# Attention with normalised q and k, then a gated MLP: another timing for the preparation of q and k and for their loads

## The chip, the cores and the metric

The kernel runs on one core of one Trainium2 chip. The metric is the device time of one execution in microseconds; the median of three executions of the kernel before was 333.86 (331.49 to 334.69). Profiles are single executions under the hardware profiler. The granted clock is the share of TensorE's full clock that it was given; the DMA share is the mean busy share of the core's 16 DMA engines as the profile counts it, and it goes above 1. PE is TensorE's matmuls and PEld its weight loads, DVE is VectorE, ACT is ScalarE, POOL is GpSimd, SP is SyncE, which here only issues transfers. An execution counts as slow when it lies more than 1.5% above the fastest execution of the same kernel in the same rounds.

## The reference, cut to what matters

```python
# q, k, v: 8 batches x 12 heads x 448 tokens x 64, float32
def rmsnorm(x, g):
    rms = np.sqrt(np.mean(x * x, axis=-1, keepdims=True) + 1e-06)
    return x / rms * g
q_n, k_n = rmsnorm(q, g_q), rmsnorm(k, g_k)
attn = softmax(q_n @ k_n.T / sqrt(64))          # per head
x = (attn @ v), heads side by side              # 8 x 448 x 768
h = relu(x @ w_in)                              # 768 x 1024
u, v = halves of h;  v_n = layernorm(v)
v_s = w_spatial @ v_n + b_spatial               # over tokens
out = (u * v_s) @ w_out                         # 512 x 768
```

## The kernel before

Each batch is cut into three groups of four heads, 24 groups in all. Raw q and k are loaded, squared, summed, turned into a scale by a logarithm and an exponential on ACT, multiplied by it, and transposed. From then on the kernel is one clock of steps. A step computes two passes of scores on PE into a single tile of PSUM and ends in one exponential on ACT; a group takes 3.5 steps. The first 20 passes go one at a time ("early passes" p0 to p19); then come steps 10 to 83, and a tail. Group G is first needed at step 3.5 G. I call "step s" the moment at which its exponential starts.

```python
def squares(*key, eng=None):                      # GpSimd, or ACT where asked
    ...
    if eng is act:
        act.activation(out=t, in_=x, func=AF.Square, bias=0.0, scale=1.0)
    else:
        pool.tensor_tensor(out=t, in0=x, in1=x, op=ALU.mult)

def reduce(*key):                                 # DVE: sum of squares -> "ms"
    dve.tensor_reduce(out=sqs[gk][:, key[1], :], in_=..., axis=AX.X, op=ALU.add)

def rstd(*gk):                                    # ACT: "ln", then "rs"
    act.activation(out=ln, in_=t, func=AF.Ln, bias=eps, scale=1.0 / D)
    act.activation(out=rst[gk], in_=ln, func=AF.Exp, bias=0.0, scale=-0.5)

def scaled(*key, eng=None):                       # GpSimd, or DVE: "n"
    (eng or pool).tensor_tensor(out=..., in0=raw[key], in1=<scale, broadcast>, op=ALU.mult)

def transpose_dma(G, i):                          # on SyncE's queue: "qT", "kr"
    sync.dma_start_transpose(out=..., in_=nrm[G, i]...)

def k_scale(G):                                   # DVE, once k's transpose has landed: "kT"
    dve.tensor_scalar(out=t, in0=krs.pop(G), scalar1=g2_col, ..., accum_out=tot)

# ... cut: loads; q and k of batches 0 and 1 come group by group ("qf", "kf": 4 pieces each),
# those of batches 2 to 7 a whole batch at a time ("qb", "kb": 4 pieces each), all on SyncE's queue

EVEN = {-8: ("sq", 0), -7: ("sq", 1), -6: ("red",), -5: ("rstd",), -4: ("sc", 1), -1: ("ks",)}
ODD = {-6: ("sq", 0), -5: ("sq", 1), -4: ("red",), -3: ("rstd",), -2: ("sc", 1), 2: ("ks",)}
# ... for G >= 6: step 7 * (G // 2) + offset, one or two later for G < 8
for b in range(2, B):
    s0 = max(S0 + 2 if b == 2 else 17, NCH * NG * b // 2 - 17)
    for n in range(8):
        at(s0 + n // (2 if b < 4 else 1), NG * b, "ld", n)

for s in range(S0, NST):
    scores(pss[:, 0:2], 2 * s)                    # PE
    scores(pss[:, 2:4], 2 * s + 1)
    prep(s, True)                                 # ACT's logarithms, before the exponential
    expo(pss, 2 * s, 2)
    prep(s, False)                                # squares, sums, scales, transposes, loads
    # ... cut: v, w_out; attention of a finished group, or units of the MLP
```

In these traces ACT, GpSimd and SyncE each take their instructions in the order of the program. So a logarithm that waits holds the next exponential (3.40 us before the one at 175.43 us in the prediction's third fence), and a square that waits holds all of GpSimd's later work (3.76 us before the one at 172.59).

## Time and profile before

| read from the profile before | value |
|---|---|
| span of the profiled execution | 333.2 us |
| first exponential / step 10 | 11.79 / 44.46 us |
| step 24 | 100.95 us |
| step 43 / step 83 | 163.51 / 302.01 us |

The starts of the exponentials are the best ruler for this kernel, since every cause of delay must show in one of them. In the lines of a timeline the first number is the start in microseconds, the second the duration, then engine, source line, operation, output and input; the bracket is the idle time of the engine just before, and what ended it. In the view of waits a line says who waited for whom, the sum in microseconds, how often, and the longest. The lines themselves are in the prediction below.

| line in the timelines | what it is |
|---|---|
| L249 | square on GpSimd |
| L257, L265, L266 | sum on DVE; logarithm and exponential that make the scale |
| L276 | multiplication by the scale |
| L340, L346 | transposing transfer; the copy of k's transpose on DVE |
| L366, L373 | scores; the step's exponential |
| L90 to L93 / L105 | load of a group / of a part of a batch |

### The profile page before, as it was taken

Reading aid. Unit: us, or ns where it says so; the run is one execution under the profiler, and the core shown is the slowest. Engines: PE = TensorE matmul, PEld = TensorE weight load, DVE = VectorE, ACT = ScalarE, POOL = GpSimd, SP = SyncE. Lnnn points to the kernel's source line nnn. Section 1 sums busy time; section 2 is a strip of 40 time slices with the busy share of each in tenths; the row PEclk is TensorE's granted clock in tenths of the full one; section 3 lists DMA queues with packets and bytes.
Section 4 is the critical chain, followed back from the end, with each engine's and each line's share of the span. In section 5 each row is a group of like instructions: output and inputs, shape, how many; then the busy total and the mean of one; then the engine's idle time right before and its main releaser. Section 6 shows DMA issues by size and latency. Waiting matters only on the chain.

```text
span 333.2 us, 6464 instructions
## 1 busy us (share of the span) xinstructions
PE 281.5 (84%) x2537; PEld 131.0 (39%) x2537; DVE 200.3 (60%) x340; ACT 212.5 (64%) x276; POOL 205.3 (62%) x183
## 2 busy tenths in 40 slices
PE   7568779739759999779977989989959989999994
PEld 7333333314314444334433434334334434444552
DVE  5784645543648394495655585586756566745652
ACT  3637766827646877658656768767755776675411
POOL 4576795659976697379545896499464990120210
PEclk9977979978997999999995999999987999999999
DMA  4999897998991999839977999589946397131155
GB/s 124 223 209 229 154 132 162 191 205 123 182 231 27 205 213 244 172 79 152 237 170 93 228 201 232 107 143 179 280 59 108 35 201 79 26 94 49 25 144 165
DMA packets 82944, 50.90 MB, mean 153 GB/s; under 512 B 46753, under 2 KB 79170, under 8 KB 82914
## 3 DMA queue, kind: packets, MB, share of 16 engines
q1 hardware_dynamic: 67218, 41.53, 61.9%
q0 software_dynamic: 15408, 8.73, 20.1%
q8 instruction: 20, 0.33, 0.4%
q10 hardware_dynamic: 288, 0.23, 0.3%
q14 instruction: 10, 0.08, 0.1%
HBM read 38.55 MB, written 11.01 MB: 149 GB/s over the span
## 4 chain that ended last, share of the span: by engine, by line
PE 32%; POOL 21%; DMA 18%; DVE 10%; issue 8%; ACT 7%; SPq 4%; POOLq 0%; DVEq 0%; ACTq 0%
POOL sqt L249 10%; DMA kb<-in_k_dram 10%; PE ps L395 8%; PE ps L526 6%; DMA kr<-n 5%; POOL n L276 5%; PE ps L467 4%; PE ps L507 4%; ACT et L373 4%; PE ps L497 3%; PE pss L366 3%; POOL vt L130 3%; DVE ms L257 3%; POOL vn L489 3%; DMA qb<-in_q_dram 2%
## 5 line engine op out<-in xcount | busy, mean ns | idle before, releaser
L373 ACT ACTIVATE et<-pss 128x1792 bf16<-128x1792 f32 x74 | 122.8, 1660 | 46.4 <-PE pss L366 42.8
L410 DVE TENSOR_TENSOR xt<-ps,rc 128x448 bf16<-128x448 f32 x48 | 28.1, 620 | 63.1 <-ACT rc L403 50.5
L366 PE MATMUL pss<-qT,kT 64*128 64x448 bf16 x254 | 38.9, 363 | 20.5 <-DVE kT L346 16.3
L257 DVE TENSOR_REDUCE ms<-sqt 128x14 f32<-128x896 f32 x46 | 48.2, 1076 | 11.3 <-POOL sqt L249 10.6
L395 PE MATMUL ps<-et,vt 128*32 128x448 bf16 x768 | 45.1, 374 | 8.6 <-DVE osb L444 7.0
L526 PE MATMUL ps<-w_out,gt 128*128 128x384 bf16 (+1 forms) x256 | 48.5, 333 | 0.3 <-DVE gt L511 0.3
L467 PE MATMUL ps<-w_in_v,xt 128*128 128x512 bf16 (+1 forms) x192 | 48.7, 393 | 0.0
L249 POOL TENSOR_TENSOR sqt<-kb 128x896 f32<-128x896 f32 x18 | 30.3, 1684 | 23.6 <-DMA kb<-in_k_dram 18.2
L497 PE MATMUL ps<-xt,w_in_u 128*128 128x448 bf16 x192 | 43.0, 369 | 1.2 <-ACT vs L436 0.7
L276 POOL TENSOR_TENSOR n<-qb,rs 128x896 bf16<-128x896 f32 x18 | 30.5, 1696 | 20.3 <-ACT rs L266 20.2
L346 DVE TENSOR_SCALAR_CACHE_REDUCE kT<-kr,g_col 128x896 bf16<-128x896 bf16 x20 | 22.7, 1137 | 22.7 <-DMA kr<-n 22.7
L395 PEld LDWEIGHTS <-vt 128*32 128x32 bf16 x768 | 23.2, 101 | 25.7 <-issue 11.7
L526 PEld LDWEIGHTS <-gt 128*128 128x128 bf16 (+1 forms) x256 | 24.6, 102 | 20.8 <-issue 7.1
L366 PEld LDWEIGHTS <-kT 64*128 64x128 bf16 x276 | 10.5, 94 | 53.1 <-issue 30.2
L444 DVE COPY osb<-ps 128x384 f32<-128x384 f32 (+1 forms) x45 | 24.4, 555 | 10.8 <-PE ps L526 7.8
L249 POOL TENSOR_TENSOR sqt<-qb 128x896 f32<-128x896 f32 x18 | 30.3, 1684 | 0.7 <-DMA qb<-in_q_dram 0.6
L276 POOL TENSOR_TENSOR n<-kb,rs 128x896 bf16<-128x896 f32 x18 | 30.4, 1691 | 0.0
L507 PE MATMUL ps<-w_spT,vn 128*128 128x448 bf16 (+1 forms) x128 | 27.2, 353 | 2.3 <-DVE w_spT L222 2.3
L485 POOL TENSOR_SCALAR nm<-mv 128x4 f32<-128x4 f32 x8 | 1.9, 237 | 43.7 <-DVE mv L476 43.6
L489 POOL TENSOR_SCALAR vn<-vs,nm,rv 128x512 bf16<-128x512 bf16 (+1 forms) x32 | 24.1, 768 | 5.4 <-ACT rv L484 4.4
L497 PEld LDWEIGHTS <-w_in_u 128*128 128x128 bf16 x192 | 17.9, 101 | 24.0 <-issue 11.5
L467 PEld LDWEIGHTS <-xt 128*128 128x128 bf16 (+1 forms) x192 | 18.2, 103 | 20.4 <-issue 6.5
(92 smaller groups left out, 354.3 us busy)
## 6 DMA issues: line engine op xcount, KB each, us to landing
out_dram<-osb SPq DMA_DIRECT2D x55, 192.0 KB, 3.9
qb<-in_q_dram SPq DMA_DIRECT2D x12, 384.0 KB, 5.8
kb<-in_k_dram SPq DMA_DIRECT2D x12, 384.0 KB, 7.2
qb<-in_q_dram SPq DMA_DIRECT2D x12, 288.0 KB, 6.5
kb<-in_k_dram SPq DMA_DIRECT2D x12, 288.0 KB, 7.3
vt<-in_v_dram POOLq DMA_DIRECT2D x16, 192.0 KB, 5.4
vt<-in_v_dram POOLq DMA_DIRECT2D x16, 144.0 KB, 5.0
qf<-in_q_dram SPq DMA_DIRECT2D x10, 128.0 KB, 4.6
```

What stands on the lines that cost most here:

```text
L249: pool.tensor_tensor(out=t, in0=x, in1=x, op=ALU.mult)
L257: dve.tensor_reduce(out=sqs[gk][:, key[1], :], in_=sqt.pop(key).rearrange("p h c d -> p (h c) d"), axis=AX.X, op=ALU.add)
L276: (eng or pool).tensor_tensor(out=t.rearrange("p c h d -> p h c d"), in0=raw[key], in1=rst[gk][:, key[1], :].rearrange("p (h c) -> p h c", ...
L366: pe.matmul(out=ps[:, h, 0:S], lhsT=kT[r, c0:c0 + 128], rhs=qT[r, :], start=True, stop=True, tile_position=(64 * h, 0))
L373: act.activation(out=ets[s][:, 2 * a:2 * a + 2 * m, :], in_=ps[:, 0:2 * m, 0:S], func=AF.Exp, bias=0.0, scale=1.0)
L395: pe.matmul(out=ps[32 * l:32 * l + 32, 0:S], lhsT=w, rhs=et_of(G, 3 if r == 3 else r + 4 * y, h), start=(r == 0), stop=(r == 3), tile_posi ...
L410: dve.tensor_tensor(out=xts[b][:, 2 * g + half, :], in0=pst.pop((G, half))[:, 0:S], in1=rec[G], op=ALU.mult)
L467: pe.matmul(out=ps[0:m, :], lhsT=xts[b][:, j, t0:t0 + m], rhs=w_in_v[:, j, :], start=(j == 0), stop=(j == 5), tile_position=(0, 0))
L489: pool.tensor_scalar(out=vn_t[b % 2][0:m, c, :], in0=vs[b][c][0:m, :], scalar1=nms[b][0:m, c:c + 1], scalar2=rvs[b][0:m, c:c + 1], op0=ALU ...
L497: pe.matmul(out=ps[:, 0:S], lhsT=w_in_u[:, j, 128 * f:128 * f + 128], rhs=xts[b][:, j, :], start=(j == 0), stop=(j == 5))
L507: pe.matmul(out=ps[:, 0:S], lhsT=vn_t[b % 2][0:kp, c, 128 * f:128 * f + 128], rhs=w_spT[0:kp, c, :], start=(c == 0), stop=(c == NT - 1))
L526: pe.matmul(out=ps[o:o + m, 0:384], lhsT=gts[b][f][:, t0:t0 + m], rhs=w_out[:, f, r], start=(f == 0), stop=(f == 3), tile_position=(0, o))
```

## The change

The intent: GpSimd should never get two squares in one step; batch 2 joins batches 0 and 1 in being loaded group by group; the order of the first groups' work is written out by hand; the loads of the other batches get more lead. The lines of the timelines keep their numbers.

```diff
-    load_first(1, 1, sync)
+    load_first(1, 1, act)
...
         if p == 0:
-            squares(1, 0, eng=act)
             squares(1, 1)
             load_v(0, range(4))
+            load_w_in(1)
+            squares(2, 1)
+            load_w_in(0)
...
+        elif p == 1:
+            squares(1, 0, eng=act)
...
         elif p == 3:
             rstd(1)
             scaled(1, 0, eng=dve)
             scaled(1, 1, eng=dve)
-            squares(2, 0)
-            squares(2, 1)
-            load_w_in(1)
+        elif p == 4:
+            squares(2, 0, eng=act)
...
+    EVEN = {"sq": (-11, -8), "red": (-9, -7), "rstd": (-6,), "sc": (-6, -5), "tr": (-5, -4), "ks": (-1,)}
+    ODD = {"sq": (-9, -7), "red": (-6, -5), "rstd": (-3,), "sc": (-3, -2), "tr": (-2, -1), "ks": (2,)}
+    FIRST = {4: {...}, 5: {"sq": (10, 11), "red": (11, 12), "rstd": (13,), "sc": (13, 14), "tr": (14, 14), "ks": (16,)},
+             6: {"sq": (13, 14), "red": (14, 15), "rstd": (16,), "sc": (16, 17), "tr": (17, 17), "ks": (20,)},
+             7: {"ldg": (12, 12), "sq": (15, 17), ..., "tr": (19, 20), "ks": (23,)},
+             8: {"ldg": (15, 15), "sq": (18, 20)}}
...
+    SC8 = 23
+    for b in range(3, B):
+        first_q = max(15 if b == 3 else SC8 + 1, (21 * b - 38) // 2)
+        for n in range(4):
+            todo.setdefault(first_q + n // 2, []).append(("ld", NG * b, n))
+            todo.setdefault(first_q + 2 + (n if b % 2 == 0 else n // 2), []).append(("ld", NG * b, n + 4))
```

The first lines move two transfers, the second half of the first k, from SyncE's queue to ACT's. The pairs are steps for q and for k. "ldg" loads a group of batch 2, "ld" a quarter of a batch's q or k. Within a step, transposes are issued before loads. Also cut: group 6 is loaded in the early passes 16 and 17, v of batch 1 is issued in pass 9 instead of 15, the loads of whole batches use their two buffers in the other order, and the buffers of the start are given up in step 24 instead of 17.

## The prediction

> **What bounds the kernel now.** I read the page first, then ACT's rows in order of time, and for each long gap all engines around it. The lines of the page that matter are the busy shares, the DMA row and the chain that ended last:
>
> ```profile
> span 333.2 us, 6464 instructions
> ...
> PE 281.5 (84%) x2537; PEld 131.0 (39%) x2537; DVE 200.3 (60%) x340; ACT 212.5 (64%) x276; POOL 205.3 (62%) x183
> ...
> PE 32%; POOL 21%; DMA 18%; DVE 10%; issue 8%; ACT 7%; SPq 4%; POOLq 0%; DVEq 0%; ACTq 0%
> ...
> L373 ACT ACTIVATE et<-pss 128x1792 bf16<-128x1792 f32 x74 | 122.8, 1660 | 46.4 <-PE pss L366 42.8
> ```
>
> No engine is full. PE looks it at 84%, but only 32% of the chain is PE; 39% is GpSimd plus DMA, which mostly prepare q and k. The kernel is a clock of 84 steps, each ending in an exponential on ACT. From step 10 (start 44.46 us) to step 83 (302.0) there are 73 steps in 257.5 us, 3.53 us each. Undisturbed runs of steps are shorter: the exponentials at 151.51 and 163.51 are four steps apart, 3.0 us each, and there PE works almost without a gap. So 3.0 us is what PE asks for, and the other 0.53 x 73 = 39 us are stalls. ACT idles 46.4 us before these 74 exponentials; this counts short waits too. The long gaps on ACT that I can name: 5.01 us at 20 us, 7.15 at step 17, 2.56 at step 20, 4.47 at step 24, 2.88 at step 35, then 3.40 + 2.58 at steps 46 and 47 and, one period of two batches later, 3.49 + 2.58 at steps 67 and 68. Sum 34.1 us. Three kinds, one of each:
>
> ```profile
> 17.33 4.55 DVE L276 TENSOR_TENSOR n<-qf,rs 128x896 bf16<-128x896 f32 x1 [0.80 <-ACT rs L266]
> 17.56 1.74 POOL L249 TENSOR_TENSOR sqt<-qf 128x896 f32<-128x896 f32 x1
> ...
> 19.20 1.73 POOL L249 TENSOR_TENSOR sqt<-kf 128x896 f32<-128x896 f32 x1
> ...
> 21.81 1.08 DVE L276 TENSOR_TENSOR n<-kf,rs 128x896 bf16<-128x896 f32 x1
> ...
> 25.24 1.73 ACT L373 ACTIVATE et<-pse 128x896 bf16<-128x896 f32 x2 [5.01 <-PE pse L366]
> ```
>
> This is the timeline (start, duration). The same DVE multiplication takes 1.08 us alone and 4.55 beside two GpSimd squares: it ends just after they do. Group 1's transposes wait for it.
>
> ```profile
> 62.95 3.36 SPq L340 DMA_TRANSPOSE kr<-n  x1
> ...
> 71.21 1.15 DVE L346 TENSOR_SCALAR_CACHE_REDUCE kT<-kr,g_col 128x896 bf16<-128x896 bf16 x1 [7.29 <-DMA kr<-n]
> ...
> 73.02 1.67 ACT L373 ACTIVATE et<-pss 128x1792 bf16<-128x1792 f32 x1 [7.15 <-PE pss L366]
> ```
>
> Second kind: group 5's transposed k is issued in the step that consumes it, and lands 8.3 us after its issue (71.21 - 62.95), behind the big loads of batches 2 and 3.
>
> ```profile
> 164.10 0.65 SPq L105 DMA_DIRECT2D kb<-in_k_dram  x1
> ...
> 172.59 1.68 POOL L249 TENSOR_TENSOR sqt<-kb 128x896 f32<-128x896 f32 x1 [3.76 <-DMA kb<-in_k_dram]
> ...
> 175.43 0.32 ACT L265 ACTIVATE ln<-ms,eps 128x28 f32<-128x28 f32 x1 [3.40 <-DVE ms L257]
> ```
>
> Third kind: the last part of batch 5's k leaves SyncE at 164.10, two steps before its square; square, sum and logarithm follow in series, and ACT holds the next exponential behind the logarithm.
>
> **What the skill says.** "SBUF — State Buffer", section "Who interferes with whom": a VectorE instruction with two SBUF inputs contends with a GpSimd instruction that reads SBUF, and the second to issue waits the first out. The 4.55 against 1.08 us agree. "DMA: Bandwidth & Descriptors", section "Issuing engines are not separate DMA queues": all queues end on the same 16 engines, so another issuer saves only issue time. Here a SyncE issue is about 0.61 us. The same page, "Queues, rings and completion order": each ring is consumed in order, so a transpose issued after loads waits behind them; the 8.3 us of k's transpose beside a median of 4.7 for such transposes agree. "Perfetto Trace Analysis", "Identifying the Most-Contended Engine", warns that matmul busy time and the occupancy of 16 DMA engines both mislead; indeed the windows view gives DMA shares above 1, up to about 1.2 in its fullest 10 us.
>
> **The change, part by part.** No computation is added; squares, sums and transposes are the same in number. One square (group 2's q) goes from GpSimd to ACT: 0.95 us (the same form at 13.46) there instead of 1.7 on GpSimd.
>
> 1. Start. Two first loads go to ACT's queue: SyncE's later loads leave 2 x 0.61 = 1.2 us earlier. Group 1's q square on ACT moves behind exponential 1, which removes its 0.77 us wait for data, but the k square still ends about 15.0, so group 1's scale is still ready at 17.3. Then the two DVE multiplications find GpSimd only issuing loads (15.0 to 19.9; at 21.81 such issuing did not stretch DVE): 2 x 1.09 instead of 4.55 + 1.08. Saved: 5.63 - 2.18 = 3.4 us, all on the path. The first attention moves one exponential later and both halves of w_in load some 3 to 12 us earlier, which I count as nothing. With earlier arrivals up to step 10: 4 us.
>
> 2. Steps 10 to 24. Batch 2's groups 6, 7, 8 come in small loads (128 and 96 KB a piece) in the order of need, and group 5 is scaled in steps 13 and 14 rather than 14 and 15, transposed in 14, used in 16: two steps (6 us) for k's transpose instead of none. Group 6's transposes move from step 19 to 17 (used in 20), group 7's from 21 to 19 and 20 (used in 23). Against 7.15 + 2.56 + 4.47 = 14.2 us of stalls I would expect 10 to 12 back if DMA were free. It isn't: the window 0 to 101 us has shares of 0.96, 1.03 and 0.99, some 100 us of sixteen engines' work. At 1.2 the same work takes 83 us, so step 24 (100.95 now) cannot come much before 85. Part 1's 4 us and this part together would ask for 85 to 87, with no slack. I take 6 us here, so 10 in sum, step 24 at about 91.
>
> 3. Steps 24 to 43. Even groups are summed, normalized and transposed a step earlier: three steps from k's transpose to its use rather than two, 9 us against the 7.4 us that group 10's took (127.59 to 135.00). That removes most of 2.88; with fewer short waits 3 us.
>
> 4. Steps 43 to 83. In odd batches k's last part is issued at step 36 instead of 42 (21 steps later for batch 7), and group 15's k is squared in step 42 instead of 44: six steps of room instead of two. That removes 3.40 + 3.49 and the 2 x 2.58 that follow from them (DVE, late by the sum, frees PE's banks late): 12.0 us. Squares and sums now sit singly in their steps (at most two GpSimd operations of 1.69 in a 3.0 us step), but GpSimd stays an in-order engine with 3 us of LayerNorm and 4 issues of v a batch, so I leave 1 us for new waits: 11 us.
>
> Sum: 10 + 3 + 11 = 24 us of 334; predicted 310. As a check, steps 24 to 83 would take 201 - 14 = 187 us for 59 steps, 3.17 each, still above 3.0.
>
> The tail after step 83, 31 us, is untouched.
>
> **Rivals.** *DMA becomes the bound.* For it: shares near 1 until 236 us; queues 61.9% + 20.1% of the span are 273 us of work that the change does not lessen. At 1.2 that is 228 us at least, and most of it must come before step 64. Against: the windows 235.8 to 333 have shares from 0.67 to 0.37, and between 137 and 163 it is 0.86, so from step 24 on there is room. If it bites through the first half, only the end of part 4 and part 1 remain: 320 to 325.
>
> *The stalls return as other waits.* The outputs stand in SyncE's queue before loads and transposes and wait for DVE's copies (51.2 us in 7 waits at one of these lines), and the logarithm of each group still blocks ACT if GpSimd is late: square to logarithm stays two steps for even groups. That would eat half: about 321.
>
> *Everything goes.* All 34 us named return, and PE, less often idle, keeps a higher clock (granted 0.91 in the stalled stretch from 163.5, 1.00 in the next): about 300. DMA speaks against it.
>
> **Range and chances.** Between the third rival and the first: 300 to 323. 2% of 333.86 is at 327.2; to stay above it two thirds of the named stalls would have to remain or be replaced. I give 0.87 to faster, 0.11 to the same and 0.02 to slower, since no work is added.
>
> **What would show it.** In the profile after: group 1's two DVE multiplications at about 1.1 us each and no 5 us gap near 20 us (part 1); step 17's gap below 3 us and step 24 near 91 (part 2); no logarithm that waits over 3 us after 160 us, and kb's last loads landed before their squares (part 4); ACT's idle before the 74 exponentials down from 46.4 to about 25. DMA shares of 1.1 and more in every window up to 90 us, with transposes landing 8 us late, would show the first rival; new waits of ACT's logarithms or of the transposes behind outputs the second. If step 24 stays near 100 or if steps 43 to 83 still take over 132 us (138.5 now), the prediction is wrong.

## The result, and the profile after

The changed kernel took 318.7 us in the median of three executions (317.55 to 318.87). The ratio of the mean of its fast executions to the mean of the fast executions of the kernel before in the same rounds is 0.9551 (95% interval 0.9467 to 0.9635); being a ratio of means over a selection, it is not quite the ratio of the medians. All ratios below are computed so. The time is inside the predicted range, 8.7 us above the 310 us predicted. The profiled executions differ by 333.2 - 316.8 = 16.4 us, where I had predicted 24.

These are lines of the page of the changed kernel: span, busy shares, the chain that ended last, and the exponentials with ACT's idle time before them.

```profile
span 316.8 us, 6478 instructions
...
PE 276.5 (87%) x2527; PEld 128.3 (40%) x2537; DVE 197.4 (62%) x340; ACT 212.2 (67%) x277; POOL 203.6 (64%) x182
...
PE 39%; POOL 15%; DMA 14%; DVE 12%; ACT 9%; SPq 5%; issue 5%; POOLq 0%; DVEq 0%; ACTq 0%
...
L373 ACT ACTIVATE et<-pss 128x1792 bf16<-128x1792 f32 x74 | 122.9, 1660 | 52.2 <-PE pss L366 48.8
```

GpSimd and DMA, 39% of the chain before, are 29% now, and PE has grown from 32 to 39%. The idle time before the exponentials did not fall: 52.2 us against 46.4. The view of waits says where it went. First before, then after:

```profile
ACT ln L265 <- DVE ms L257: 24.4, 18, 3.5
DVE kT L346 <- DMA kr<-n: 22.7, 8, 7.3
POOL sqt L249 <- DMA kb<-in_k_dram: 18.2, 5, 6.5
```

```profile
DVE ms L257 <- POOL sqt L249: 17.3, 8, 3.9
...
POOL sqt L249 <- DMA kb<-in_k_dram: 9.6, 1, 9.6
DVE kT L346 <- DMA kr<-n: 9.5, 2, 6.8
ACT ln L265 <- DVE ms L257: 7.0, 7, 1.8
```

Logarithms used to stop ACT for 24.4 us in 18 waits; now it is 7.0. An idle moment that began before a logarithm now begins before the exponential that follows, so the sum in the exponential's row is no measure of what was gained. The starts of the exponentials are. The table subtracts them in the two profiles.

| | before | after | gain so far | gain of the part | predicted |
|---|---|---|---|---|---|
| step 10 | 44.46 | 44.38 | 0.1 | 0.1 | 4 |
| step 24 | 100.95 | 97.65 | 3.3 | 3.2 | 6 |
| step 43 | 163.51 | 159.73 | 3.8 | 0.5 | 3 |
| step 83 | 302.01 | 285.66 | 16.4 | 12.6 | 11 |
| end | 333.16 | 316.79 | 16.4 | 0.0 | 0 |

**The start.** The timeline of the changed kernel from 14.5 us on, group 1's squares and multiplications:

```profile
15.10 1.67 POOL L249 TENSOR_TENSOR sqt<-kf 128x896 f32<-128x896 f32 x1 [4.59 <-DMA kf<-in_k_dram]
...
18.54 1.09 DVE L276 TENSOR_TENSOR n<-qf,rs 128x896 bf16<-128x896 f32 x1 [0.64 <-ACT rs L266]
...
19.33 2.32 POOL L198 DMA_DIRECT2D w_in_v<-in_moe_w_in_dram  x4
...
19.55 2.57 DVE L276 TENSOR_TENSOR n<-kf,rs 128x896 bf16<-128x896 f32 x1
...
24.48 2.54 ACT L373 ACTIVATE et<-pse 128x896 bf16<-128x896 f32 x3 [2.71 <-PE pse L366]
```

The first multiplication is down from 4.55 to 1.09 us, as intended. But the k square starts at 15.10, where before it started at 13.30, since its data landed later. And the second multiplication takes 2.57 us beside GpSimd's issues of w_in (19.33 to 21.65). The early pass p7 comes at 24.48 instead of 25.24. The first attention, now a pass later, moves its gap with it (p9 to p10 took 3.22 us before, p10 to p11 takes 2.98 now), so compare around it: p11 is 1.0 us ahead (30.35 against 31.35), p19 0.8. Of that, 0.7 is lost before step 10, where the sum of group 4's q now stands in the way (a wait of 1.35 us before, 2.06 after).

**Steps 16 to 21.** The timeline from 58 to 88 us:

```profile
60.09 1.24 SPq L340 DMA_TRANSPOSE kr<-n  x1
...
66.00 1.66 ACT L373 ACTIVATE et<-pss 128x1792 bf16<-128x1792 f32 x1
66.34 0.60 SPq L93 DMA_DIRECT2D kf<-in_k_dram  x1
66.99 2.61 SPq L105 DMA_DIRECT2D qb<-in_q_dram  x4
...
72.99 3.48 SPq L340 DMA_TRANSPOSE kr<-n  x1
...
83.80 1.15 DVE L346 TENSOR_SCALAR_CACHE_REDUCE kT<-kr,g_col 128x896 bf16<-128x896 bf16 x1 [6.81 <-DMA kr<-n]
...
85.99 1.66 ACT L373 ACTIVATE et<-pss 128x1792 bf16<-128x1792 f32 x1 [7.36 <-PE pss L366]
```

The exponential at 66.00 is step 17, and its wait of 7.15 us is gone: group 5's k was issued at 60.09, two steps ahead. At step 20 the kernel is 8.4 us ahead (76.96 against 85.38). Then a wait of the old size stands in another place, step 21 at 85.99: group 6's k was issued at 72.99 and had landed only when DVE took it at 83.80, 10.8 us later. Ahead of it in SyncE's queue are four loads of batch 3's q ("qb", x4) and the loads of group 8. The windows view of the changed kernel gives, for a stretch of time, its length, then busy time of PE, PEld, DVE, ACT and GpSimd with counts, the granted clock, the DMA share and GB/s:

```profile
44.00:66.00 22.00, 20.19 (x169) 7.74 (x171) 14.05 (x24) 17.22 (x23) 17.35 (x13) 0.84 0.64 140
66.00:85.40 19.40, 12.03 (x114) 5.51 (x113) 7.61 (x13) 9.64 (x12) 17.61 (x16) 0.84 1.31 183
```

The DMA share is 0.64 just before group 6's transposes are issued, and 1.31 while they are awaited. The granted clock is 0.62 from 85.4 to 90.6 us, just after this wait, and step 22 took 4.71 us.

**Steps 43 to 48.** The timeline from 160 us on:

```profile
167.09 0.32 ACT L265 ACTIVATE ln<-ms,eps 128x28 f32<-128x28 f32 x1
167.76 1.66 ACT L373 ACTIVATE et<-pss 128x1792 bf16<-128x1792 f32 x1
...
171.50 1.66 ACT L373 ACTIVATE et<-pss 128x1792 bf16<-128x1792 f32 x1 [1.03 <-PE pss L366]
```

The logarithm before step 46 no longer waits (3.40 us before), and step 47 waits 1.03 instead of 2.58 us. Steps 46 and 47 took 6.04 and 5.27 us before, 2.71 and 3.74 now; steps 67 and 68 repeat it, 6.13 and 5.26 before, 2.71 and 3.74 now.

### The profile page after: what moved, and what is told of

It is laid out like the page before. It is cut to its first block, busy times and chain, and to the rows that moved or that the text cites. A ratio compares the mean times of both kernels' runs of the same rounds, so it can differ in the third digit from the quotient of the medians.

```text
span 316.8 us, 6478 instructions
## 1 busy us (share of the span) xinstructions
PE 276.5 (87%) x2527; PEld 128.3 (40%) x2537; DVE 197.4 (62%) x340; ACT 212.2 (67%) x277; POOL 203.6 (64%) x182
## 4 chain that ended last, share of the span: by engine, by line
PE 39%; POOL 15%; DMA 14%; DVE 12%; ACT 9%; SPq 5%; issue 5%; POOLq 0%; DVEq 0%; ACTq 0%
PE ps L526 10%; PE ps L467 7%; POOL sqt L249 6%; ACT et L373 6%; PE ps L507 6%; PE pss L366 6%; PE ps L395 6%; DMA kb<-in_k_dram 4%; POOL n L276 4%; PE ps L497 4%; DVE ms L257 4%; DMA qf<-in_q_dram 3%; POOL vn L489 3%; DMA kf<-in_k_dram 2%; DMA kr<-n 2%
## 5 line engine op out<-in xcount | busy, mean ns | idle before, releaser
L373 ACT ACTIVATE et<-pss 128x1792 bf16<-128x1792 f32 x74 | 122.9, 1660 | 52.2 <-PE pss L366 48.8
L257 DVE TENSOR_REDUCE ms<-sqt 128x14 f32<-128x896 f32 x46 | 49.3, 1075 | 17.9 <-POOL sqt L249 17.3
L467 PE MATMUL ps<-w_in_v,xt 128*128 128x512 bf16 (+1 forms) x182 | 45.4, 381 | 0.4
L395 PE MATMUL ps<-et,vt 128*32 128x448 bf16 x768 | 44.1, 369 | 1.7 <-ACT lr L402 1.7
L276 POOL TENSOR_TENSOR n<-qb,rs 128x896 bf16<-128x896 f32 x15 | 25.4, 1693 | 25.4 <-ACT rs L266 25.3
L497 PE MATMUL ps<-xt,w_in_u 128*128 128x448 bf16 x192 | 40.3, 354 | 0.8 <-ACT vs L436 0.8
L366 PEld LDWEIGHTS <-kT 64*128 64x128 bf16 x276 | 10.8, 94 | 51.3 <-issue 31.1
L249 POOL TENSOR_TENSOR sqt<-kb 128x896 f32<-128x896 f32 x15 | 25.1, 1682 | 9.6 <-DMA kb<-in_k_dram 9.6
L395 PEld LDWEIGHTS <-vt 128*32 128x32 bf16 x768 | 21.3, 101 | 20.0 <-issue 6.4
L507 PE MATMUL ps<-w_spT,vn 128*128 128x448 bf16 (+1 forms) x128 | 28.1, 364 | 0.1
L497 PEld LDWEIGHTS <-w_in_u 128*128 128x128 bf16 x192 | 17.3, 98 | 21.2 <-issue 7.5
L276 POOL TENSOR_TENSOR n<-kb,rs 128x896 bf16<-128x896 f32 x15 | 25.4, 1693 | 0.1
L249 POOL TENSOR_TENSOR sqt<-qb 128x896 f32<-128x896 f32 x15 | 25.2, 1678 | 0.0
```

Source lines behind the costliest of these rows:

```text
L257: dve.tensor_reduce(out=sqs[gk][:, key[1], :], in_=sqt.pop(key).rearrange("p h c d -> p (h c) d"), axis=AX.X, op=ALU.add)
L276: (eng or pool).tensor_tensor(out=t.rearrange("p c h d -> p h c d"), in0=raw[key], in1=rst[gk][:, key[1], :].rearrange("p (h c) -> p h c", ...
L366: pe.matmul(out=ps[:, h, 0:S], lhsT=kT[r, c0:c0 + 128], rhs=qT[r, :], start=True, stop=True, tile_position=(64 * h, 0))
L373: act.activation(out=ets[s][:, 2 * a:2 * a + 2 * m, :], in_=ps[:, 0:2 * m, 0:S], func=AF.Exp, bias=0.0, scale=1.0)
L395: pe.matmul(out=ps[32 * l:32 * l + 32, 0:S], lhsT=w, rhs=et_of(G, 3 if r == 3 else r + 4 * y, h), start=(r == 0), stop=(r == 3), tile_posi ...
L467: pe.matmul(out=ps[0:m, :], lhsT=xts[b][:, j, t0:t0 + m], rhs=w_in_v[:, j, :], start=(j == 0), stop=(j == 5), tile_position=(0, 0))
```

## The experiments

Theory: the gain after step 43 comes from the earlier loads of the later batches, and the missing gain before it from two orders that the change itself sets: the load that moved to ACT's queue, and batch 3's loads standing before group 6's transposes. Rivals: the gain comes from the spread squares; step 21's wait is chance; or the sixteen DMA engines are simply full.

**The changed kernel again** (x1, no edit).

> The changed kernel once more, as a control beside the others. Expected 0.955 of the kernel before, within 0.01; its profile should show the same step starts (step 24 near 97.7 us, step 43 near 159.7, step 83 near 285.7), and again a stall of about 7 us before step 21. If the stall at step 21 is a chance of one execution, it will be missing or far smaller here.

Measured: 317.82 us in the median of four (312.89 to 320.02); the ratio of 0.9373 (0.928 to 0.9466) rests on two fast executions, since one fell to 312.89, and the profiled one is slow against it. The profile again waits 6.40 us before step 21. The wait is no chance, the ratio lies outside the 0.945 to 0.965 expected (0.944 with all four executions), and executions of this kernel spread by 7 us. One part of the spread shows: step 12 takes 3.00 us here and 5.33 in the first profile, where the clock from 47 to 52 us is 0.52 (1.00 in x1). Step 10 to step 24 takes 50.63 us here, 53.27 there.

**Only the new loads** (x2): the kernel before, with the new load steps of batches 4 to 7 and nothing else.

```diff
+        first_q = max(24, (21 * b - 38) // 2)
         for n in range(8):
-            at(s0 + n // (2 if b < 4 else 1), NG * b, "ld", n)
+            if b < 4:
+                at(s0 + n // 2, NG * b, "ld", n)
+            elif n < 4:
+                at(first_q + n // 2, NG * b, "ld", n)
+            else:
+                at(first_q + 2 + (n - 4 if b % 2 == 0 else (n - 4) // 2), NG * b, "ld", n)
```

> The kernel before with one part of the change alone: the issue steps of the loads of batches 4 to 7. Theory (the gain of steps 43 to 83 comes from k's loads leaving earlier): steps 43 to 83 take 126 to 129 us instead of 138.5, no logarithm waits over 2.5 us in that stretch, the total falls by 9 to 13 us, ratio 0.96 to 0.975. Rival (the gain comes from spreading squares and sums over single steps, and one step more for the transposes): steps 43 to 83 stay over 135 us, ratio 0.985 to 1.0. The head up to step 24 is as before in both.

Measured: 325.41 us (324.62 to 326.29), ratio 0.9679 (0.964 to 0.9718). Steps 43 to 83 take 129.35 us instead of 138.5. The same place as in the prediction's third fence, from this run's timeline:

```profile
168.05 1.68 POOL L249 TENSOR_TENSOR sqt<-kb 128x896 f32<-128x896 f32 x1
...
171.30 0.32 ACT L265 ACTIVATE ln<-ms,eps 128x28 f32<-128x28 f32 x1 [0.63 <-DVE ms L257]
...
175.50 1.66 ACT L373 ACTIVATE et<-pss 128x1792 bf16<-128x1792 f32 x1 [1.03 <-PE pss L366]
```

The square no longer waits for its load (3.76 us before) and the logarithm waits 0.63 instead of 3.40. The moved loads alone give 9 of the 12.6 us (129.35 is just above the 126 to 129 expected).

**The changed kernel with the old offsets** of squares, sums, scales and transposes for groups 8 to 23 (x3).

```diff
-    EVEN = {"sq": (-11, -8), "red": (-9, -7), "rstd": (-6,), "sc": (-6, -5), "tr": (-5, -4), "ks": (-1,)}
-    ODD = {"sq": (-9, -7), "red": (-6, -5), "rstd": (-3,), "sc": (-3, -2), "tr": (-2, -1), "ks": (2,)}
+    EVEN = {"sq": (-8, -7), "red": (-6, -6), "rstd": (-5,), "sc": (-5, -4), "tr": (-4, -3), "ks": (-1,)}
+    ODD = {"sq": (-6, -5), "red": (-4, -4), "rstd": (-3,), "sc": (-3, -2), "tr": (-2, -1), "ks": (2,)}
```

> The changed kernel with the old step tables of squares, sums and scaling for groups 8 to 23, all loads and the first groups as changed: the complement of the run before this one. Theory (loads matter, spreading hardly): within 3 us of the changed kernel, ratio 0.955 to 0.965; the even groups' transposes of k have two steps again, so a wait of 1 to 3 us may come back at step 35. Rival (spreading matters): 8 us or more slower than the changed kernel, ratio 0.98 or more.

Measured: 318.17 us (315.98 to 319.31), ratio 0.9455 (0.9404 to 0.9506), the same as the changed kernel's. Steps 43 to 83 take 130.5 us, against 125.9 to 127.6 in all eleven profiles with the new offsets; so the spread is worth some 2 to 4 us in that stretch (x2, without it as well, took 129.35). In the total it does not show: step 24 comes at 94.34 here, at 97.65 and 95.48 in the changed kernel's two profiles. The wait before step 21 is 8.92 us.

**Batch 3's loads three steps earlier** (x4), into the emptier stretch before 66 us.

```diff
-        first_q = max(15 if b == 3 else SC8 + 1, (21 * b - 38) // 2)
+        first_q = 12 if b == 3 else max(SC8 + 1, (21 * b - 38) // 2)
```

> The changed kernel with batch 3's loads three steps earlier (q in steps 12 and 13, k in 14 and 15 instead of 15 to 18), into the stretch from 50 to 67 us in which the DMA share is only about 0.7. Theory (group 6's transposed k lands late because the burst of batch 3 is ahead of it in SyncE's ring, while the DMA engines stood half idle just before): the wait before step 21 falls from 7.4 to under 3 us, step 24 comes 3 to 7 us earlier than 97.7, ratio 0.935 to 0.947. Rival (the DMA engines are simply full through the head, the order makes no difference): another transpose or load waits instead, step 24 within 2 us of 97.7, ratio 0.95 to 0.96.

Measured: 317.01 us (315.25 to 317.91), ratio 0.9437 (0.9395 to 0.948); step 24 at 95.93. My expectation of the waits was a miss: step 21 still waits 4.08 us, and the wait of step 17 is back. From the timeline:

```profile
63.18 2.80 SPq L340 DMA_TRANSPOSE kr<-n  x1
...
71.83 1.66 ACT L373 ACTIVATE et<-pss 128x1792 bf16<-128x1792 f32 x1 [7.58 <-PE pss L366]
```

Now group 5's transpose is issued behind the burst (56.5 to 59.9 us). In these two orders the wait belongs to the transpose that follows the burst.

**Batch 3's loads between the transposes** (x5): q in step 11 behind group 4's transposes, k in halves behind group 5's and group 6's.

```diff
+            if b == 3:
+                todo.setdefault(11, []).append(("ld", NG * b, n))
+                todo.setdefault((14, 14, 17, 17)[n], []).append(("ld", NG * b, n + 4))
+                continue
```

> The changed kernel with batch 3's loads put between the transposes instead of in front of them: its q right behind group 4's transposes (step 11), half of k behind group 5's (step 14), the other half behind group 6's (step 17). The run with the loads three steps earlier only moved the wait: its burst stood in front of group 5's transposed k, and step 17 waited 7.6 us instead. Theory (the place in SyncE's ring against the next transposes decides): no wait over 3 us at steps 17 and 21, step 24 at 90 to 94 us, total 4 to 7 us below the changed kernel, 311 to 314. Rival (the head has too many bytes; whatever goes first, something lands late): a wait of 4 us or more stays at step 17, 21 or 24, step 24 at 95 or later, total within 3 us of the changed kernel.

Measured: 313.6 us (312.06 to 314.52), ratio 0.9376 (0.9326 to 0.9427). Its timeline:

```profile
64.81 1.22 SPq L340 DMA_TRANSPOSE kr<-n  x1
...
69.39 1.66 ACT L373 ACTIVATE et<-pss 128x1792 bf16<-128x1792 f32 x1 [4.03 <-PE pss L366]
...
74.80 1.29 SPq L340 DMA_TRANSPOSE kr<-n  x1
...
81.92 1.66 ACT L373 ACTIVATE et<-pss 128x1792 bf16<-128x1792 f32 x1 [2.10 <-PE pss L366]
```

Step 21's wait falls to 2.10 us and step 24 comes at 92.38. Step 17 waits 4.03, because SyncE slowed down ahead of group 5's transposes: with eight loads under way, it issued the next only when the oldest had landed (issues at 58.10, 60.08 and 61.44, landings at 58.09, 60.07 and 61.42). This wait is over the 3 us that I expected and just over the rival's 4; step 24 and the total came out as the theory has them. The same bytes in another order save 3 to 5 us of the total: against x8 below, which is nearly the changed kernel and ran in the same rounds, 4.7 in the medians and 3.6 in the means.

**w_out later** (x6): its 1.57 MB (as read in float32; 768 KB in bfloat16 as written) leave the crowded stretch.

```diff
-        if s == 18:
+        if s == 24:
             load_w_out()
```

> The changed kernel with w_out's load (768 KB, 12 us to land in the changed kernel's fullest stretch) in step 24 instead of 18. By the byte rival, the wait before step 21 shrinks by some 2 to 3 us, since w_out's packets share the engines with group 6's transposes, and the total by 2 to 3 us. By the ring-order theory, the transposed k of group 6 is issued at 73 us, before w_out at 75.6, and waits for SyncE's own earlier loads; the wait shrinks by under 1.5 us and the total stays within 2 us.

Measured: 325.11 us (323.79 to 326.06), ratio 0.9722 (0.967 to 0.9775). Step 21 still waits 7.08 us, so the bytes of w_out are not what that transpose waits for. As a version it is my error: w_out is needed right after step 24, and PE waited for it:

```profile
103.29 0.48 PE L526 MATMUL ps<-w_out,gt 128*64 128x384 bf16 x1 [10.63 <-DMA w_out<-in_moe_w_out_dram]
```

**The first k's second half back on SyncE's queue** (x7).

```diff
-    load_first(1, 1, act)
+    load_first(1, 1, sync)
```

> The changed kernel with the first k's second half back on SyncE's queue. Theory (issuing more loads at once made the first pieces land later: first q 5.98 against 5.39, group 1's k 14.9 against 13.1): the first exponential starts at about 11.8 instead of 12.9, group 1's k lands about 13.5, exponential 7 about 1 us earlier; total 0 to 1.5 us less, as the head waits for data again later. Rival (the issue time saved on SyncE helps): total 1 us more.

Measured: 315.15 us (314.39 to 317.2), ratio 0.9436 (0.9394 to 0.9479). The first exponential is at 11.80 us again, p7 at 22.48 (24.48 after), step 10 at 42.28. The four kernels with this edit (x7, x9, x10, x12) have their first exponential at 11.73 to 11.80, all the others of the changed start at 12.53 to 13.05. By step 10 the four are at 41.44 to 44.04, and those with the load on ACT's queue and no other edit of the start (the changed kernel, x1, x3 to x6) at 42.91 to 44.98: 1.4 us in the means, with overlap. The total is 3.1 us below x8's median in the same rounds, but 1.6 in the means, so I can't say whether it is more than the 0 to 1.5 expected. (x1's median is 2.7 us higher, but in other rounds, in which the kernel before was 1.7 us slower too.)

**The sum of group 4's q back in step 10** (x8).

```diff
-        elif p == 19:
-            reduce(4, 0)
...
-    FIRST = {4: {"red": (None, 10), ...
+    FIRST = {4: {"red": (10, 10), ...
```

> The changed kernel with the sum of group 4's q back in step 10, behind group 3's transposes, instead of before them. In the changed kernel that sum (1.08 us on DVE at 41.7) stands before the copies of group 3's transposes, and step 10 waits 2.06 us where the kernel before waited 1.35. Theory: that wait falls to about 1.3 and step 10 starts 0.7 us earlier, but the logarithm of group 4 then waits about 1 us more in step 11: step 12 unchanged within 1 us, total within 1 us. Rival (the wait at step 10 is lost time): total 0.7 us or more less.

Measured: 318.27 us (312.64 to 319.65; four of six executions are slow against the 312.64). Step 10's wait is 1.35 us again, but the total cannot be told from the changed kernel's within this spread. Not resolved, as expected.

**The two mends together** (x9): the edits of x5 and x7.

> Two mends of the changed kernel in one: batch 3's loads placed behind the transposes as in x5_after_b3_between (q at step 11, halves of k at steps 14 and 17), and the second half of the first k back on SyncE's queue as in x7_after_fy_sync. If the two costs are separate (start of the kernel; order in SyncE's ring at step 21), the gains add: x5 gave about 4.5 us, x7 about 2.5, so 310.5 to 312.5, first exponential at 11.8 us, step 24 at 89 to 91. If both only shift work into the same next wait, it stays at 313 to 314, and the wait at step 17 grows beyond the 4.03 of x5.

Measured: 312.22 us (309.76 to 314.08), ratio 0.9348 (0.9299 to 0.9398). Step 24 comes at 91.64, a little later than the 89 to 91 expected; step 17 waits 3.69 us, and the total is inside the 310.5 to 312.5 expected. The gains add at best partly: 1.4 us below x5 in the medians of different rounds, with overlapping ranges.

**Loads spread further** (x10): the edit of x7, and

```diff
+            if b == 3:
+                todo.setdefault((11, 11, 14, 14)[n], []).append(("ld", NG * b, n))
+                todo.setdefault((17, 17, 18, 18)[n], []).append(("ld", NG * b, n + 4))
+                continue
...
-             7: {"ldg": (12, 12), ...
+             7: {"ldg": (12, 14), ...
-             8: {"ldg": (15, 15), ...
+             8: {"ldg": (15, 17), ...
```

> As x9_fy_between, but the loads are spread more evenly between the transposes: q of batch 3 half at step 11 and half at 14, its k half at 17 and half at 18; group 7's k loads at step 14 rather than 12, group 8's k at 17 rather than 15, so that at most eight loads stand ahead of any transpose in the ring. Ring-order theory: the wait at step 17 (4.03 in x5) falls below 2 and step 21 stays below 3; step 24 at 87 to 90, total 308 to 311. Rival, that the sixteen engines are simply full up to step 24: the wait moves to a square or transpose of groups 7 to 9 (steps 20 to 26), and the total is not below x9.

Measured: 315.77 us (311.62 to 317.38), ratio 0.9388 (0.9327 to 0.9448) from the fast ones; the profiled execution is slow. Step 17's wait is gone, step 21 waits 1.96 us, step 23 comes at 86.80, and then:

```profile
83.68 4.73 SPq L340 DMA_TRANSPOSE kr<-n  x1
...
94.12 1.66 ACT L373 ACTIVATE et<-pss 128x1792 bf16<-128x1792 f32 x1 [5.17 <-PE pss L366]
```

The wait has moved to group 7's k at step 24, behind batch 3's k (issued 75.0 to 77.0) and beside w_out. The total is not below x9: the rival's sign.

**GpSimd quiet beside group 1's multiplications** (x11): w_in is issued after group 3's squares, and ACT squares group 2's k.

```diff
-            load_w_in(1)
-            squares(2, 1)
-            load_w_in(0)
...
+        elif p == 5:
+            squares(2, 1, eng=act)
...
             squares(3, 1)
+            load_w_in(1)
+            load_w_in(0)
             load_v(1, range(4))
```

> Group 1's second DVE multiplication took 2.57 us in the changed kernel beside nothing but GpSimd's issues of w_in. Here GpSimd has nothing to do between the issues of v and group 2's scaling: w_in's issues come after group 3's squares, and group 2's k square is done by ACT. If GpSimd's issuing stretched it, the multiplication takes 1.1 us, the seventh early exponential comes about 1.0 to 1.5 us earlier (less what ACT's extra square of 0.95 costs). If it still takes 2.57, GpSimd is not the cause (rival: what ACT or the arriving loads do to the memory). Total within 2 us of the changed kernel, 316 to 320, in both cases.

Measured: 319.85 us (318.98 to 320.86), ratio 0.9587 (0.9539 to 0.9635). The two multiplications in its timeline:

```profile
17.85 1.09 DVE L276 TENSOR_TENSOR n<-qf,rs 128x896 bf16<-128x896 f32 x1 [0.64 <-ACT rs L266]
...
18.86 1.08 DVE L276 TENSOR_TENSOR n<-kf,rs 128x896 bf16<-128x896 f32 x1
```

With GpSimd idle the second takes 1.08 us, although ACT squares beside it as in the changed kernel. So what GpSimd does stretched it, by 1.5 us. It is the issues of w_in: in the changed kernel GpSimd's next square starts at 21.59, when an unstretched multiplication would have ended at 20.63, and w_in's data land from 26.19 on. All eleven profiles of the changed start other than x11's show 2.57 us there. p7 comes at 21.79 instead of 24.48; 0.7 of these 2.7 us are an earlier scale. The gain is lost at step 10, which waits 7.66 us: v's later issues wait for the late w_in, and group 3's multiplication stands behind them on GpSimd (it starts at 40.12). What exactly GpSimd holds stays open: in the kernel before, the same multiplication took 1.08 us at 21.81 beside the same issues of w_in, which had begun 0.99 us ahead of it there, and 0.21 to 0.73 us ahead in the eleven profiles. In x11 itself a later multiplication takes 1.09 us at 33.39 beside them.

**Spread loads, w_out early** (x12): x10 with w_out's load in step 11.

> x10_fy_spread had neither the wait at step 17 nor a long one at step 21, and reached step 23 at 86.8 us, but then waited 5.2 us at step 24 for group 7's transposed k, issued at 83.7 us behind the second half of batch 3's k and beside w_out. Here the same, with w_out's 1.57 MB moved from step 18 to step 11, into the stretch from 44 to 66 us whose DMA share was only 0.81. If the sixteen engines are full from 66 to 88 us, taking w_out out of there lets the transposes of group 7 land some 4 us earlier: wait at step 24 below 2.5, step 25 at 93 to 96 (99.1 in x10), total 308 to 312. If the order in SyncE's ring alone sets it, step 24 waits 5 us again and the total stays at 314 to 317; a wait at step 17 of over 2 us would say that w_out now delays group 5's transposes.

Measured: 313.25 us (311.23 to 314.83), ratio 0.9354 (0.9306 to 0.9402); profiled at 309.5. Step 17 waits 1.47 us, step 21 3.12, step 24 2.64 (just above the 2.5 expected), step 25 comes at 93.44. From step 10 to step 24 it takes 48.98 us where x10 takes 51.05 and the kernel before 56.49; x9 takes 47.60. So taking w_out's bytes out of the stretch mends what x10 had made worse, and fullness seems to have a part at step 24 (one profile of each, x10's a slow one), but the even spread does not beat x9. The DMA share from 66 to 85.4 us is 1.33, not below x10's 1.22, though it moves fewer GB/s (190 against 209): the share does not measure fullness. The total is above the 308 to 312 expected.

x9 and x12 are the fastest versions, each at 0.935 of the kernel before, against 0.955 for the change itself in its own rounds and 0.944 for all of x1. x9 beats both kernels with two small edits, though one of the changed kernel's seven executions (312.89) lies in x9's range.

## Why the prediction was right or wrong

The class (faster by over 2%) and the range were right. By its own steps:

**Part 1, the start, failed: 4 us predicted, 0.1 measured** (-0.5 to 1.6 in the six profiles with just this start: the changed kernel, x1, x3 to x6). Two terms. "The k square still ends about 15.0, so group 1's scale is still ready at 17.3" was wrong: it ended at 16.77 (15.10 + 1.67) and the scale came at 18.28 to 18.51. I had counted the saved issue time of SyncE and not looked at what lands later. With the two transfers on ACT's queue the last piece of the first k's first half lands at 6.85 instead of 6.02; GpSimd squares it and only then issues group 1's k, at 8.01 instead of 7.18, and that lands at 14.94 instead of 13.13. A part of this last difference can be chance: in x2, whose start is unedited, it lands at 15.09. x7, which undoes the move, has 6.03, 7.18 and 13.26, and its first exponential at 11.80 instead of 12.86. "2 x 1.09 instead of 4.55 + 1.08" was half right: 1.09 + 2.57, so 2.0 us saved and not 3.4. I had taken one sighting of 1.08 beside GpSimd's issues as a rule; x11 shows 1.08 with GpSimd idle. The 4.55 was no constant either: x2, with the start of the kernel before, has 1.15 + 2.56 there. And "the 4.55 against 1.08 us agree" holds for the contention, not for who waits: the multiplication started at 17.33, 0.23 us ahead of the first square, and still was the one stretched. In these two profiles the sum closes: 2.0 saved, 1.2 lost by the later scale, leaves 0.8 (p7 is 0.76 us ahead), and 0.7 goes at step 10. That it closes to 0.1 is luck, since step 10 moves by 2 us between profiles with the same start. "The first attention moves one exponential later ... which I count as nothing" was right.

**Part 2, steps 10 to 24: 6 us predicted, 3.2 measured in the first profile and 5.9 in the second (56.49 - 50.63, x1).** The size was about right, by a wrong route, so that it came near was luck. By my own sign it was a miss: step 24 at 97.65 is nearer to "near 100" than to 91. The wait of step 17 went and that of step 20 shrank (8.4 us ahead at step 20, more than the 6 I took for the whole part). The limit was named wrongly: I held the first rival, the transfers' work at a share of 1.2, for the bound that keeps step 24 at 91. The trace has a share of 0.64 just before the new wait, and 1.2 is no ceiling: the kernel before has 1.26 from 120 to 130 us, the changed one 1.56 from 76 to 85.4. What took the gain back is a new wait that I had not listed, group 6's transpose behind loads of batch 3 in the same queue, 7.36 us at step 21. I had written for group 5 that a transpose waits behind loads, and did not check the same for group 6 in the new order. That the order makes it is shown: the wait recurs (x1), does not move with w_out (x6), moves to step 17 when the burst moves there (x4), and shrinks to 2.10 when the loads stand between the transposes (x5). With both orders mended, step 24 comes at 91.64 (x9) and 90.42 (x12), so the 10 us of parts 1 and 2 were there to be had. Beyond that the rival gets its share: with these waits removed or shortened, x10 has one of 5.17 us at step 24, and x12 keeps 1.47, 3.12 and 2.64.

**Part 3, steps 24 to 43: 3 us predicted, 0.5 measured.** "That removes most of 2.88" failed: step 35 still waits 2.45 us (0.93 in x1). The lines of the changed kernel's timeline:

```profile
121.72 1.75 SPq L340 DMA_TRANSPOSE kr<-n  x1
...
129.33 1.15 DVE L346 TENSOR_SCALAR_CACHE_REDUCE kT<-kr,g_col 128x896 bf16<-128x896 bf16 x1 [2.74 <-DMA kr<-n]
...
131.13 1.66 ACT L373 ACTIVATE et<-pss 128x1792 bf16<-128x1792 f32 x1 [2.45 <-PE pss L366]
```

Group 10's k was ready at 118.07, but its transpose left at 121.72: SyncE first issued four outputs (at 117.88, 118.39, 119.07 and 120.11). The last of them and the transpose left just when older loads of batch 4's k had landed (at 120.09 and 121.66). So the second rival, outputs standing in the queue before transposes, came true here; no run tests it. Besides, step 39 takes 4.41 us instead of 2.89. That is the clock: the step takes 2.89 us in the seven profiles in which it has a clock of 1.00, and 4.34 to 4.57 in six others in which, as here, it is between 0.62 and 0.67. What sets it off in some executions stays open. The variants without an error of placing need 60.0 to 62.6 us for this stretch (62.56 before).

**Part 4, steps 43 to 83: 11 us predicted, 12.6 measured.** Right, in mechanism and size. The loads carry it: 9 us with loads alone (x2). The spread of the squares, which gives the change its name, adds 2 to 4 us here and does not show in the total (x3). Parts 3 and 4 together, "187 us for 59 steps" from step 24 to 83, took 188.0; that their errors, 2.5 us too few and 1.6 too many, nearly cancel is luck. The second rival's new logarithm waits did not come: 24.4 us fell to 7.0.

**The tail** is 31.1 us in both, as said. **ACT's idle time** before the exponentials was forecast at 25 us and is 52.2; that test was ill chosen, since waits of logarithms (17 us fewer) turn into waits of exponentials.

## What to carry to other kernels

In a queue that issues in order, as SyncE's does here, a transpose that is needed soon should be issued before a burst of loads, not behind it, and after moving a burst one must look again at every transpose that now follows it, not only at the one that was late. Give loads their lead time first: here it was worth more than spreading an engine's work evenly. A first load that is moved to another queue to save issue time can land later, so compare landings and not issues.

## What the Trainium skill lacked or had wrong

- "SBUF — State Buffer", section "Who interferes with whom", infers that a multiplication of two SBUF tensors on VectorE does not contend with GpSimd's descriptor generation. The changed kernel's took 2.57 us beside GpSimd's issues of w_in, as in ten other profiles of the changed start, and 1.08 us with GpSimd idle (x11). It is not settled, since the kernel before has 1.08 beside such issues, and x11 1.09 later on.
- "DMA: Bandwidth & Descriptors", section "Queues, rings and completion order", gives ring order, which agrees with all runs (of the 166 to 180 landings of SyncE's transfers that each of the fourteen profiles shows, none is out of the order of issue), but says nothing of what a backlog does to the issuer. In these traces a transpose's issue takes SyncE 1.22 to 1.33 us with little ahead of it and up to 7.80 behind a burst (at 80.21 us in the changed kernel). In x5 a load leaves only when an older one lands, and in all fourteen profiles no load or transpose left SyncE with more than seven earlier ones seen to be under way (24 to 26 landings in each are not in the trace, so the true bound may be a little higher).
- No page gives the delay of a first load moved to ACT's queue: here the first exponential came 1.06 us later (12.86 against 11.80 in x7), and the median time was 3.1 us longer (x8 against x7, same rounds; x8 differs by one sum as well).
